# Fused attention and two MLPs on one core: other token chunks, weight decoding on another engine, a new written order

## The chip, the cores and the metric

The kernel runs on one core of a Trainium2 chip. The core has a matrix engine (PE; its weight loads are told apart as PEld), a vector engine (DVE), an activation engine (ACT), a general engine (POOL) and a queue that issues DMAs (SP). Each takes its instructions strictly in the order in which they stand in its own queue; semaphores join the queues. The metric is the device time of one execution in microseconds (us). Three runs of the kernel before took 647.95, 648.45 and 654.52; the median is 648.45.

## The reference

Three layers follow each other; all is float32, but `moe_w_in` and `moe_w_out` arrive as float64.

```python
# attention: q, k, v of shape (2, 8, 576, 64)
q_d, k_d, v_d = means over groups of 4 positions          # 144 of them
out_d   = softmax(q_d k_d^T / 8) v_d, each row repeated 4 times
out_loc = softmax(q k^T / 8, only where |i - j| < 4) v
x = (out_d + out_loc), as 1152 tokens x 512
# first MLP: w_in 512 x 2048, w_out 2048 x 512
h = x @ w_in;  x = (h * sigmoid(h)) @ w_out
# four experts: w1 512 x 1024, w2 1024 x 512 each, p = normalised domain_probs
out = sum over e of p[:, e] * (relu(x @ w1[e]) @ w2[e])
```

## The kernel before, in words

**Products.** Every float32 operand of the two MLPs is split into a high and a low part (fp32r tiles), and each product is three matmuls: high by high, high by low, low by high (`mm3`, L601). A weight tile is 128x128; the moving operand is a chunk of tokens.

**Attention** is 16 jobs of 256 or 320 tokens (two batches, two token halves, four pairs of heads), each a chain over several engines. The program has a name for every step: S (local scores, PE), x (row maximum and subtraction, DVE), e (exp, ACT), D (scores of the averaged positions, PE), n (their maximum, DVE), d (their exp, ACT), u (row sums, DVE), r and g (normalising, DVE and ACT), T (transposes, PE), a (copies, ACT), V (products with the values, PE), o, f, h, l (the two parts of x). k, v, p, tp are sums over four positions on POOL, q the same on DVE. M are the first matmuls of the first MLP.

**First MLP.** The 2048 hidden columns are done in two halves (hf 0 and 1) of 1024. Each half goes over four chunks of tokens. For a chunk, G (8 column tiles x 4 depth steps x 3 matmuls = 96) makes h; th, gf, gh, gl evacuate it (tanh on ACT, product on DVE, the two parts on ACT and DVE); H (4 x 8 x 3 = 96 matmuls) multiplies with `w_out`; ya adds it to the result. G2_3_1 is chunk 2, column tile 3, depth step 1; chunks 4 to 7 are those of the second half. Chunks 0 and 1 of the first half are worked in `quarter` (L660), so that they can begin while attention still runs; the others in the loop at L1054. Three banks of PSUM (`mm_p`, L68) hold sums.

**Weights of the first MLP** come as float64, in 32 pieces of 128x512 (s0 to s31, 512 KB each) into three staging buffers (`stg_p`, L75; a few in `acc`). `split_raw` (L226) turns a piece into its two float32 parts: A (ACT) rescales the high word into a tile `dec`; B (DVE, a shift) or Z (ACT, from the upper half of the low word) makes the three bits that are missing; C (DVE) joins them; w (ACT) makes the high part, L (POOL) the low part by a difference. B is used for the pieces in `LOW_ON_DVE` (L55), Z for the others. Pieces 0 to 15 serve the first half and 16 to 31 the second.

**The order.** The order on each engine up to the second half is written out by hand: five lists of step names (`WRITTEN`, L931), for SP, PE, ACT, DVE and POOL. Each step of a list is made to follow the one before it on its engine. DMAs have eight completion semaphores in turn, so an issue in SP's queue waits until the DMA eight places earlier or more on the same semaphore has landed.

**Experts** follow (L808 to L928). Nothing of them is changed.

Of the kernel before, what the change touches and what calls it, by code (L numbers as in the profile page):

```python
# [62 lines left out]
def attention_moe_kernel(ctx, tc, kqa, kqb, qtl, va, vb, w64, w1d, w2d, dpr, out):  # L63
# [596 lines left out]
    def quarter(ci, p, o, n):  # L660
        c = slice(o, o + n)
        g = [4 * ci + i for i in range(4)]
        two = n == 256
# [15 lines left out]
        for sums in groups:
            first = {}  # L680
            for i in range(4):
                wh, wl = parts(2 + p, i)
                for d, ps in sums:
                    if not two or len(sums) == 4:
                        next_step(0.125)
                    s = slice(d * 128, d * 128 + 128)
                    h, l = gh[g[i]][:, 0:n], gl[g[i]][:, 0:n]
                    for x, (a, y) in enumerate(((wh, h), (wh, l), (wl, h))):
                        z = two and d % 2
                        m = PE.matmul(out=ps[:, 0:n], lhsT=a[:, s], rhs=y, start=(not z and i == 0 and x == 0),  # L690
                                      stop=(i == 3 and x == 2), skip_group_check=True)
                        if i == 0 and x == 0:
                            first[d] = m
                            if z:
                                after(m, first[d - 1])
                        mark(f"H{ci}_{d}_{4 * p + i}", m)
                if i:
                    attn_tick()
            for d, ps in sums:
                ya = acc[:, d * NT + o:d * NT + o + n]  # L700
                if p == 0:
                    i = ACT.activation(out=ya, in_=ps[:, 0:n], func=ACTF.Copy, scale=0.5)
                else:
                    i = DVE.scalar_tensor_tensor(out=ya, in0=ps[:, 0:n], scalar=0.5, in1=ya, op0=ALU.mult, op1=ALU.add)
                mark(f"ya{ci}_{d}_{p}", i)
# [192 lines left out]
    def outputs(e, ci, ch, p):  # L898
# [33 lines left out]
        """in_kq0 in_kq1 in_s0 in_kq2 in_vg0 in_kq3 in_vg1 in_kq4 in_kq5 in_vw0 in_s1 in_qt in_vg3 in_vw1 in_s3 in_vg2 in_vw2  # L932
        in_s2 in_kq6 in_s8 in_s10 in_vw3 in_kq7 in_s9 in_vg8 in_vw4 in_kq12 in_vw5 in_kq8 in_s11 in_vg9 in_kq9 in_s4
        in_vw6 in_vw7 in_kq10 in_kq11 in_s5 in_vw8 in_s6 in_vw9 in_vg10 in_vg11 in_kq13 in_vw10 in_s7 in_vw11 in_s12
        in_s13 in_qt1 in_kq14 in_s14 in_s15 in_kq15 in_s16 in_s17 in_vw12 in_s18 in_vw13 in_vw14 in_vw15 in_s19 in_s20
        in_s21 in_s22 in_s23 in_pr in_s24 in_s25 in_s26 in_s27 in_s28 in_s29 in_s30 in_s31 in_w8_0 in_w8_1 in_w9_0""",
        """S0 S1 D0 D1 S2 S3 T0 D2 S4 V0 S5 T1 D3 D5 D4 V1 M0 T2 M1 V2 T3 tD S6 T4 V3 D6 S7 M2 tT M3 V4 T5 D7 S8 T6 V5 D8
        H0_0_0 H0_2_0 H0_3_0 S9 H0_1_0 H0_0_1 H0_2_1 V6 T7 G1_0_0 H0_1_1 D9 H0_3_1 G1_0_1 G1_0_2 V7 S10 H0_0_2 H0_2_2 T8
        H0_3_2 G1_0_3 S11 H0_2_3 H0_3_3 H0_1_2 G1_1_0 G1_1_1 D10 G1_1_2 G1_1_3 H0_0_3 V8 T9 D11 G1_2_0 G1_2_1 G1_2_2
        G1_3_0 G1_2_3 H0_1_3 G1_3_1 G1_3_2 G1_3_3 S12 H1_0_0 H1_0_1 H1_1_0 V9 T10 H1_1_1 H1_2_0 H1_2_1 H1_2_2 H1_0_2  # L940
        H1_0_3 H1_2_3 H1_1_2 H1_1_3 H1_3_0 G0_4_0 H1_3_1 G0_4_1 G0_4_2 H1_3_2 D12 G0_4_3 G0_5_0 G0_5_1 G0_5_2 H1_3_3 V10
        S13 G0_5_3 G0_6_0 G0_6_1 G0_7_0 G0_6_2 G0_6_3 G0_7_1 T11 H0_0_4 H0_2_4 G0_7_2 H0_1_4 G0_7_3 V11 T12 utD D13 G1_4_0
        G1_4_1 G1_4_2 G1_4_3 S14 H0_0_5 H0_3_4 G1_5_0 H0_1_5 H0_2_5 H0_0_6 H0_1_6 G1_5_1 G1_5_2 H0_3_5 G1_5_3 H0_2_6 S15
        H0_3_6 H0_0_7 H0_2_7 G1_6_0 H0_3_7 G1_6_1 H0_1_7 utT D15 D14 G1_6_2 G1_6_3 G1_7_0 G1_7_1 G1_7_2 G1_7_3 H1_0_4 V12
        T13 H1_1_4 H1_1_5 H1_0_5 H1_2_4 H1_2_5 H1_1_6 H1_0_6 H1_1_7 H1_2_6 H1_2_7 H1_3_4 H1_0_7 G2_0_0 G2_0_1 G2_0_2
        G2_1_0 G2_0_3 V13 T14 G2_1_1 G2_1_2 G2_1_3 G2_2_0 H1_3_5 G2_2_1 G2_2_2 G2_2_3 H1_3_6 V14 T15 G2_3_0 G2_4_0 G2_3_1
        G2_3_2 G2_4_1 H1_3_7 G2_4_2 G2_3_3 G2_4_3 V15 G2_5_0 G2_5_1 G2_5_2 G2_6_0 G2_7_0 G2_5_3 G2_7_1 G2_7_2 G2_6_1
        G2_6_2 G2_6_3 H2_0_0 H2_0_1 H2_0_2 G2_7_3 H2_1_0 H2_1_1 H2_0_3 H2_1_2 H2_1_3 H2_1_4 H2_0_4 H2_2_0 H2_0_5 H2_2_1
        H2_1_5 H2_0_6 H2_1_6 H2_2_2 H2_2_3 H2_2_4 H2_1_7 H2_0_7 H2_2_5 H2_3_0 H2_3_1 G3_0_0 H2_3_2 H2_2_6 H2_2_7 H2_3_3
        G3_0_1 H2_3_4 G3_0_2 G3_0_3 G3_1_0 H2_3_5 G3_1_1 G3_1_2 G3_1_3 G3_2_0 G3_2_1 G3_2_2 H2_3_6 G3_3_0 G3_2_3 H2_3_7  # L950
        G3_3_1 G3_3_2 G3_3_3 G3_4_0 G3_4_1 G3_4_2 G3_4_3 G3_5_0 G3_5_1 G3_5_2 G3_5_3 G3_6_0 G3_6_1 G3_6_2 G3_7_0 G3_7_1
        G3_6_3 G3_7_2 H3_0_0 G3_7_3 H3_0_1 H3_1_0 H3_0_2 H3_1_1 H3_1_2 H3_0_3 H3_0_4 H3_1_3 H3_2_0 H3_1_4 H3_2_1 H3_2_2
        H3_2_3 H3_1_5 H3_0_5 H3_0_6 H3_1_6 H3_0_7 H3_1_7 H3_2_4 H3_2_5 H3_2_6 H3_3_0 H3_2_7 H3_3_1 G4_0_0 G4_0_1 G4_0_2
        G4_0_3 H3_3_2 G4_1_0 H3_3_3 G4_1_1 G4_1_2 H3_3_4 H3_3_5 H3_3_6 G4_1_3 G4_2_0 H3_3_7 G4_2_1 G4_2_2 G4_2_3 G4_3_0
        G4_4_0 G4_3_1 G4_3_2 G4_3_3 G4_5_0 G4_5_1 G4_4_1 G4_4_2 G4_5_2 G4_5_3 G4_4_3 G4_6_0 G4_6_1 G4_6_2 G4_6_3 G4_7_0
        G4_7_1 H4_0_0 H4_0_1 H4_0_2 G4_7_2 H4_1_0 H4_1_1 G4_7_3 H4_0_3 H4_1_2 H4_0_4 H4_1_3 H4_0_5 H4_2_0 H4_0_6 H4_2_1
        H4_0_7 H4_1_4 H4_2_2 H4_1_5 H4_3_0 H4_3_1 H4_1_6 H4_3_2 H4_2_3 H4_3_3 H4_2_4 H4_1_7 H4_3_4 H4_2_5 H4_3_5 H4_3_6
        H4_2_6 H4_2_7 H4_3_7""",
# [243 lines left out]
```

## Time and profile before

| | |
|---|---|
| median of three runs | 648.45 us |
| the profiled execution | 649.48 us |
| its span (first to last instruction) | 647.7 us |
| PE busy | 629.0 us, 97% of the span |
| DVE, ACT, POOL busy | 64%, 50%, 38% |
| chain that ended last | PE 94%, DVE 3%, ACT 2%, DMA 1% |

The profile's page gives busy times and a chain of work followed back from the last instruction. Matmuls are pipelined: one lasts longer than the distance to the next, so the pace of PE is read from start to start, or from a run of matmuls in the chain divided by their number. A row of a timeline gives the start, the length, the engine, the line, what is written and read, the shape, how many instructions were merged, and in brackets the engine's idle time before it and what ended it.

### The profile page before, as it was taken

To read this page: it belongs to the slowest core of one execution; us is meant where nothing else is said; L and a number is where in the kernel's file an instruction comes from. 1 tells how busy PE (TensorE), PEld (TensorE's weight loads), DVE (VectorE), ACT (ScalarE), POOL (GpSimd) and SP (SyncE) were. 2 spreads that over 40 slices of the span, in tenths; PEclk is the share of its full clock that TensorE was granted. 3 is DMA by queue.
4 is the path that set the end of the run, shared out by engine and by line. 5 is a ranking of instruction groups with operands and counts; after the bars stand their busy time and mean duration, and the time that the engine had idled before them with its cause. 6 is when DMAs were issued, how large, how long until landed. Compare 5 with 4: busy or idle time off the path is not lost.

```text
span 647.7 us, 13723 instructions
## 1 busy us (share of the span) xinstructions
PE 629.0 (97%) x5492; PEld 617.6 (95%) x5492; DVE 415.4 (64%) x859; ACT 325.3 (50%) x746; POOL 249.1 (38%) x353
## 2 busy tenths in 40 slices
...
GB/s 276 285 164 187 175 173 56 78 100 163 194 2 1 132 1 1 162 67 2 1 34 108 113 9 1 1 67 131 66 1 2 1 66 1 1 33 35 2 32 50
DMA packets 16928, 48.17 MB, mean 74 GB/s; under 512 B 2976, under 2 KB 4256, under 8 KB 16864
## 3 DMA queue, kind: packets, MB, share of 16 engines
...
## 4 chain that ended last, share of the span: by engine, by line
PE 94%; DVE 3%; ACT 2%; DMA 1%; issue 0%; POOL 0%; ACTq 0%
PE mm L603 57%; PE p L864 27%; PE mm L690 4%; PE s L403 2%; PE o L522 1%; PE t L490 1%; PE o L518 1%; DVE acc L892 1%; DMA kq<-in_kqa_dram 1%; PE mm L993 1%; PE s L410 1%; PE s L448 0%; PE t L492 0%; ACT dec L236 0%; PE mm L403 0%
## 5 line engine op out<-in xcount | busy, mean ns | idle before, releaser
L603 PE MATMUL mm<-xh,wbuf 128*128 128x256 f32 (+2 forms) x1248 | 259.6, 292 | 0.0
L603 PEld LDWEIGHTS mm<-xh,wbuf 128*128 128x128 f32 x1248 | 203.7, 188 | 0.1
L603 PE MATMUL mm<-xl,wbuf 128*128 128x256 f32 (+2 forms) x624 | 182.0, 292 | 0.0
L849 POOL TENSOR_TENSOR r<-r 128x128 f32<-128x128 f32 x160 | 95.0, 606 | 177.4 <-ACT r L843 133.1
L852 DVE TENSOR_TENSOR h<-r,h 128x384 fp32r<-128x384 f32 (+1 forms) x128 | 91.6, 718 | 65.7 <-ACT h L851 65.4
L851 ACT ACTIVATE h<-r 128x384 fp32r<-128x384 f32 (+1 forms) x128 | 73.3, 578 | 93.5 <-POOL r L849 54.5
L603 PEld LDWEIGHTS mm<-xl,wbuf 128*128 128x128 f32 x624 | 117.1, 188 | 0.0
L864 PE MATMUL p<-wext,h 128*128 128x256 f32 x672 | 89.2, 276 | 0.0
L864 PE MATMUL p<-wbuf,h 128*128 128x256 f32 x672 | 82.7, 276 | 0.0
L864 PEld LDWEIGHTS p<-wext,h 128*128 128x128 f32 x672 | 82.2, 188 | 0.0
L864 PEld LDWEIGHTS p<-wbuf,h 128*128 128x128 f32 x672 | 79.4, 188 | 0.0
L603 PE MATMUL mm<-gh,wbuf 128*128 128x256 f32 (+2 forms) x384 | 77.1, 292 | 0.0
L603 PEld LDWEIGHTS mm<-gh,wbuf 128*128 128x128 f32 x384 | 62.0, 188 | 0.0
L843 ACT ACTIVATE r<-mm 128x512 f32<-128x512 f32 x48 | 28.6, 596 | 65.4 <-PE mm L603 64.7
L849 DVE TENSOR_TENSOR r<-r 128x128 f32<-128x128 f32 x96 | 39.3, 410 | 34.0 <-ACT r L843 29.4
L603 PE MATMUL mm<-gl,wbuf 128*128 128x256 f32 (+2 forms) x192 | 55.8, 291 | 0.0
L631 DVE TENSOR_TENSOR gl<-gf,gh 128x256 fp32r<-128x256 f32 (+2 forms) x64 | 34.2, 540 | 18.1 <-ACT gh L630 17.7
L625 DVE SCALAR_TENSOR_TENSOR gf<-th,mm 128x256 f32<-128x256 f32 (+2 forms) x64 | 28.7, 451 | 23.6 <-ACT th L624 21.6
L251 POOL TENSOR_TENSOR wbuf<-dec,wbuf 128x512 fp32r<-128x512 f32 x24 | 31.0, 1301 | 26.4 <-ACT wbuf L250 20.4
L892 DVE SCALAR_TENSOR_TENSOR acc<-p,pr,acc 128x256 f32<-128x256 f32 (+1 forms) x63 | 36.1, 605 | 3.6 <-PE p L864 3.0
L794 POOL TENSOR_TENSOR wext<-kst,wext 128x512 fp32r<-128x512 f32 x8 | 10.4, 1300 | 69.5 <-ACT wext L792 46.9
L630 ACT ACTIVATE gh<-gf 128x256 fp32r<-128x256 f32 (+2 forms) x64 | 28.0, 442 | 16.5 <-DVE gf L625 15.7
(173 smaller groups left out, 1035.2 us busy)
## 6 DMA issues: line engine op xcount, KB each, us to landing
...
```

The costliest lines, as they stand in the source:

```text
L251: mark(f"L{4 * u + j}", POOL.tensor_tensor(out=l, in0=d, in1=h.bitcast(F32), op=ALU.subtract))
L603: ins = [PE.matmul(out=ps, lhsT=l, rhs=r, start=(first and i == 0), stop=(last and i == n - 1)) for i, (l, r) in enumerate(pairs)]
L625: mark(f"gf{c}_{ft}", DVE.scalar_tensor_tensor(out=gf[:, 0:n], in0=th[:, 0:n], scalar=1.0, in1=ps[:, 0:n], op0=ALU.add, op1=ALU.mult))
L630: latest[ACT] = mark(f"gh{c}_{ft}", ACT.activation(out=gh[g][:, 0:n], in_=gf[:, 0:n], func=ACTF.Copy))
L631: latest[DVE] = mark(f"gl{c}_{ft}", DVE.tensor_tensor(out=gl[g][:, 0:n], in0=gf[:, 0:n], in1=gh[g][:, 0:n].bitcast(F32), op=ALU.subtract))
L690: m = PE.matmul(out=ps[:, 0:n], lhsT=a[:, s], rhs=y, start=(not z and i == 0 and x == 0), stop=(i == 3 and x == 2), skip_group_check=True)
L843: ACT.activation(out=r[:, 0:4].rearrange("p s t -> p (s t)"), in_=ps[:, 0:512], func=ACTF.Relu)
L849: latest[eng] = eng.tensor_tensor(out=r[:, o], in0=r[:, a], in1=r[:, b], op=op)
L851: ACT.activation(out=h, in_=r[:, part], func=ACTF.Copy)
L852: latest[DVE] = DVE.tensor_tensor(out=l, in0=r[:, part], in1=h.bitcast(F32), op=ALU.subtract)
L864: ins = [PE.matmul(out=ps, lhsT=x, rhs=y, start=(opens and k == 0 and i == 0), stop=(k == 3 and i == n - 1), skip_group_check=True) for i, ...
L892: DVE.scalar_tensor_tensor(out=o, in0=ps, scalar=p, in1=o, op0=ALU.mult, op1=ALU.add)
```

## The change

1. `CHUNKS`: both halves now use chunks of 256, 256, 256 and 384 tokens; the first half had 256, 320, 256 and 320. `quarter` loses its code for 320 tokens: both its chunks sum two column blocks in one PSUM bank. The pools of gh, gl, th and gf are 256 wide until the last chunk of the first half, and 384 wide from there (they were 320 wide until the second half).
2. `LOW_ON_DVE` has pieces 16 to 31 too: their missing bits are made by the shift B on DVE, and Z leaves ACT. For these pieces `dec` is no tile of its own any more: A writes over the high word in the staging buffer, and C, w and L work there.
3. The five lists of `WRITTEN` are new.

```diff
-XN = (256, 320, 256, 320)
-CHUNKS = (tuple(zip(XOFF, XN)), ((0, 256), (256, 256), (512, 256), (768, 384)))
+CHUNKS = ((0, 256), (256, 256), (512, 256), (768, 384))
...
-LOW_ON_DVE = (0, 1, 2, 3)
+LOW_ON_DVE = (0, 1, 2, 3) + tuple(range(16, 32))
...
-            d = d_p.tile([128, 512], F32, tag="dec", name="dec")
+            d = d_p.tile([128, 512], F32, tag="dec", name="dec") if u < 4 else v[:, :, 1].bitcast(F32)
...
-        if two:
-            b = [mm_tile() for _ in range(2)]
-            groups = [[(d, half(b[d // 2], d % 2)) for d in range(4)]]
-        else:
-            groups = [[(d, mm_tile()) for d in ds] for ds in ((0, 1, 2), (3,))]
+        b = [mm_tile() for _ in range(2)]
+        sums = [half(b[d // 2], d % 2) for d in range(4)]
...
-        """in_kq0 in_kq1 in_s0 in_kq2 in_vg0 in_kq3 in_vg1 in_kq4 in_kq5 in_vw0 in_s1 in_qt in_vg3 in_vw1 in_s3 in_vg2 in_vw2
+        """in_kq0 in_kq1 in_s0 in_kq2 in_kq3 in_vg0 in_s1 in_kq4 in_s2 in_vg1 in_vw0 in_vw1 in_qt in_kq5 in_vw2 in_vw3 in_vg2
...
-        """e0 A0 e1 d0 d1 e2 g0 a0 tab w0 o0 d2 g1 e3 A1 h0 e4 e5 a1 w1 d3 o1 d4 g2 h1 a2 d5 g3 A2 g4 A3 o2 a3 Z8 w3 h2 g5
+        """tab e0 A0 d0 g0 e1 w0 e2 A1 a0 e3 d1 g1 d2 o0 e4 w1 h0 a1 d3 d4 g2 e5 o1 a2 h1 Z10 A2 d5 g4 g3 o2 a3 A3 g5 w2 h2
...
+            if hf == 0 and lastc:
+                m1ctx.close()
+                open_g(384)
```

The built programs show what the new lists do. ACT at the start of the program, before:

```order
L424 ACT_TABLE_LOAD
L424 ACTIVATE s<-s 128x280
L236 ACTIVATE dec<-stg_136 128x512
L424 ACTIVATE s<-s 128x280
L465 ACTIVATE ed,s<-s,stf 128x144 x2
L424 ACTIVATE mm<-mm 128x280
L480 ACTIVATE ed<-ed,stf 128x144
```

and after:

```order
L294 ACT_TABLE_LOAD
L294 ACTIVATE qdl<-zero 128x128
L422 ACTIVATE s<-s 128x280
L234 ACTIVATE dec<-stg_136 128x512
L463 ACTIVATE ed,s<-s,stf 128x144
L478 ACTIVATE ed<-ed,stf 128x144
L422 ACTIVATE s<-s 128x280
```

A small fill of `qdl`, which needs only a zeroed column, now stands first; the load of the table goes with it, ahead of the first exp (e0) and no longer behind job 0's maximum. Job 0's d and g stand ahead of job 1's exp.

SP at the start (kq: keys and queries of a job, stg: a weight piece, vg and vw: values, qt: queries of the tail), before:

```order
L128 DMA kq<-in_kqa_dram 128x838 x2
L128 DMA stg_136<-in_w_dram 128x512
L128 DMA kq_f<-in_kqa_dram 128x838
L128 DMA vg_f_147<-in_va_dram 72x1024
L128 DMA acc<-in_kqa_dram 128x838
L128 DMA vg_f_153<-in_va_dram 72x1024
L128 DMA kq<-in_kqb_dram 128x646 x2
L128 DMA vw<-in_va_dram 72x512
L128 DMA stg_138<-in_w_dram 128x512
```

and after:

```order
L126 DMA kq<-in_kqa_dram 128x838 x2
L126 DMA stg_136<-in_w_dram 128x512
L126 DMA kq_f<-in_kqa_dram 128x838
L126 DMA acc<-in_kqa_dram 128x838
L126 DMA vg_f_147<-in_va_dram 72x1024
L126 DMA stg_138<-in_w_dram 128x512
L126 DMA kq<-in_kqb_dram 128x646
L126 DMA stg_140<-in_w_dram 128x512
L126 DMA vg_f_153<-in_va_dram 72x1024
L126 DMA vw<-in_va_dram 72x512 x2
```

Pieces s1 and s2 moved ahead of the values vw0 of job 0; kq5 moved behind them.

DVE up to f0 (the L527 or L525 instruction, which makes job 0's part of x), before:

```order
L478 TENSOR_TENSOR sm<-s,stf 128x280
L418 TENSOR_REDUCE stf<-mm 128x4
L419 TENSOR_TENSOR mm<-mm,stf 128x280
L463 TENSOR_REDUCE stf<-mm 128x1
L464 TENSOR_SCALAR stf<-stf 128x1
L418 TENSOR_REDUCE st<-s 128x5
L419 TENSOR_TENSOR s<-s,st 128x350
L527 TENSOR_TENSOR o<-o,od 128x256
L427 TENSOR_REDUCE mm<-mm 128x4
L239 TENSOR_SCALAR stg_138<-stg_138 128x512
```

and after:

```order
L242 SCALAR_TENSOR_TENSOR dec<-dec,stg_138 128x512
L237 TENSOR_SCALAR stg_140<-stg_140 128x512
L425 TENSOR_REDUCE s<-s 128x4
L461 TENSOR_REDUCE stf<-mm 128x1
L462 TENSOR_SCALAR stf<-stf 128x1
L469 TENSOR_SCALAR s<-s 128x5
L470 RECIPROCAL stf<-s 128x5
L476 TENSOR_TENSOR sm<-s,stf 128x280
L416 TENSOR_REDUCE st<-s 128x5
L417 TENSOR_TENSOR s<-s,st 128x350
L425 TENSOR_REDUCE mm<-mm 128x4
L525 TENSOR_TENSOR o<-o,od 128x256
```

The decoding of pieces 1 and 2 (B and C at L237 and L242, here of stg_138 and stg_140) stood behind f0 and now stands ahead of it; B2 is the L237 row of stg_140.

## Rows read from the trace of the kernel before

**Rows 1.** Stages: window, length, busy (count) by engine, PE clock, DMA share, GB/s.

```profile
4.00:24.00 20.00, 15.21 (x162) 11.31 (x162) 14.19 (x37) 8.05 (x22) 12.04 (x23) 0.83 0.99 296
24.00:42.00 18.00, 15.65 (x197) 13.96 (x195) 15.35 (x48) 15.13 (x44) 13.72 (x18) 0.91 0.68 226
42.00:130.00 88.00, 87.35 (x1001) 82.03 (x1000) 61.68 (x160) 65.18 (x182) 34.85 (x53) 1.00 0.44 136
130.00:175.00 45.00, 45.00 (x339) 44.96 (x339) 23.16 (x40) 35.76 (x74) 20.63 (x16) 1.00 0.51 156
```

**Rows 2.** Timeline of PE: S0, D0, T0, V0's value products, M0, M3's last.

```profile
4.37 1.20 PE L403 MATMUL s<-kq 64*64 64x70 f32 x16 [4.37 <-DMA kq<-in_kqa_dram]
...
8.76 0.74 PE L444 MATMUL s<-kd,qp 64*64 64x144 f32 x4 [1.37 <-ACT s L424]
...
15.02 0.63 PE L490 MATMUL t<-ident,sm 128*70 128x128 f32 x4 [1.88 <-DVE sm L478]
...
19.97 1.07 PE L522 MATMUL o<-at,vw 70*64 70x64 f32 x16
...
26.15 0.39 PE L993 MATMUL mm<-xh,wbuf 128*128 128x256 f32 x1
...
42.26 0.28 PE L993 MATMUL mm<-xh,wbuf 128*128 128x256 f32 x1
```

**Rows 3.** The chain: start, length, work; matmuls of 320, 256 and 384 columns.

```profile
108.57 5.29 PE mm L690 x36
...
302.90 2.72 PE mm L603 x24
...
328.40 4.16 PE mm L603 x24
```

**Rows 4.** Groups by form: the first and last of six with 320-column matmuls.

```profile
L603 PE MATMUL mm<-xh,wbuf 128*128 128x320 f32 x128 | 32.0, 312 | 0.0
...
L690 PE MATMUL mm<-gl,wbuf 128*128 128x320 f32 x32 | 10.0, 312 | 0.0
```

**Rows 5.** Lines L239 (B) and L244 (C): count, least, median and greatest ns.

```profile
L239 DVE TENSOR_SCALAR stg<-stg x3: 421/426/1241, 10.0 to 32.1; 128x512 int32<-128x512 int32 x3
...
L244 DVE SCALAR_TENSOR_TENSOR dec<-dec,stg x29: 679/691/1565, 11.4 to 171.6; 128x512 int32<-128x512 int32 x29
```

**Rows 6.** Groups by form: Z, A and L.

```profile
L251 POOL TENSOR_TENSOR wbuf<-dec,wbuf 128x512 fp32r<-128x512 f32 x24 | 31.0, 1301 | 26.4 <-ACT wbuf L250 20.4 <-DVE st L463 5.5
...
L236 ACT ACTIVATE dec<-stg 128x512 f32<-128x512 f32 x29 | 19.4, 669 | 1.8 <-POOL wext L251 0.8 <-DMA stg<-in_w_dram 0.3 <-POOL wbuf L251 0.3
...
L242 ACT ACTIVATE stg<-stg 128x512 int32<-128x512 uint16 x26 | 17.4, 674 | 2.2 <-DMA stg<-in_w_dram 2.2
```

**Rows 7.** Timeline of ACT: the table load.

```profile
6.97 1.28 ACT L424 ACT_TABLE_LOAD   x1 [6.97 <-DVE s L419]
```

**Rows 8.** Timeline of SP: the issues of s1 and of s2.

```profile
7.30 0.33 SPq L128 DMA_DIRECT2D stg<-in_w_dram  x1
...
15.49 0.35 SPq L128 DMA_DIRECT2D stg<-in_w_dram  x1
```

**Rows 9.** Timeline of DVE: f0, x6's second instruction, l3.

```profile
21.34 0.43 DVE L527 TENSOR_TENSOR o<-o,od 128x256 f32<-128x256 f32 x1 [0.66 <-ACT od L525]
...
34.64 0.53 DVE L419 TENSOR_TENSOR s<-s,st 128x350 f32<-128x350 f32 x1
...
38.13 0.41 DVE L535 TENSOR_TENSOR xl<-o,xh 128x256 fp32r<-128x256 f32 x1
```

**Rows 10.** Timelines of PE, from a matmul of H to one of V.

```profile
51.19 0.28 PE L690 MATMUL mm<-gh,wbuf 128*128 128x256 f32 x1
51.40 0.50 PE L518 MATMUL o<-atd,vd 72*64 72x80 f32 x8
```

**Rows 11.** Timelines of POOL and DVE at 10 us: a value sum beside B0.

```profile
9.96 1.04 POOL L342 TENSOR_TENSOR vg_f<-vg_f 72x512 f32<-72x512 f32 x1 [1.52 <-DMA vg_f<-in_va_dram]
...
10.04 1.24 DVE L239 TENSOR_SCALAR stg<-stg 128x512 int32<-128x512 int32 x1
```

More of the change, by code (lines that the diff above doesn't have):

```diff
@@ L672, in quarter @@
         flush()
-        if two:
-            b = [mm_tile() for _ in range(2)]
-            groups = [[(d, half(b[d // 2], d % 2)) for d in range(4)]]
-        else:
-            groups = [[(d, mm_tile()) for d in ds] for ds in ((0, 1, 2), (3,))]
-        step[0] -= 0.5
[L679 to L705, printed above, removed]
@@ new lines, in quarter @@
+        b = [mm_tile() for _ in range(2)]
+        sums = [half(b[d // 2], d % 2) for d in range(4)]
+        step[0] -= 0.5
+        first = {}
+        for i in range(4):
+            wh, wl = parts(2 + p, i)
+            for d, ps in enumerate(sums):
+                next_step(0.125)
+                s = slice(d * 128, d * 128 + 128)
+                h, l = gh[g[i]], gl[g[i]]
+                for x, (a, y) in enumerate(((wh, h), (wh, l), (wl, h))):
+                    m = PE.matmul(out=ps, lhsT=a[:, s], rhs=y, start=(d % 2 == 0 and i == 0 and x == 0),
+                                  stop=(i == 3 and x == 2), skip_group_check=True)
+                    if i == 0 and x == 0:
+                        first[d] = m
+                        if d % 2:
+                            after(m, first[d - 1])
+                    mark(f"H{ci}_{d}_{4 * p + i}", m)
+            if i:
+                attn_tick()
@@ L707, in g2_evac @@
+        for d, ps in enumerate(sums):
+            ya = acc[:, d * NT + o:d * NT + o + n]
+            if p == 0:
+                i = ACT.activation(out=ya, in_=ps, func=ACTF.Copy, scale=0.5)
+            else:
+                i = DVE.scalar_tensor_tensor(out=ya, in0=ps, scalar=0.5, in1=ya, op0=ALU.mult, op1=ALU.add)
+            mark(f"ya{ci}_{d}_{p}", i)
     def g2_evac(hf, db, c, ps, n):
@@ L936, in attention_moe_kernel @@
[L936 to L940, printed above, removed]
@@ new lines, in attention_moe_kernel @@
+        G4_4_0 G4_4_1 G4_4_2 H3_3_4 G4_5_0 G4_5_1 G4_5_2 G4_5_3 G4_4_3 H3_3_5 H3_3_6 H3_3_7 G4_6_0 G4_6_1 G4_6_2 G4_6_3
+        G4_7_0 G4_7_1 G4_7_2 G4_7_3 H4_0_0 H4_0_1 H4_0_2 H4_1_0 H4_1_1 H4_1_2 H4_0_3 H4_2_0 H4_1_3 H4_2_1 H4_0_4 H4_1_4
+        H4_2_2 H4_1_5 H4_0_5 H4_0_6 H4_1_6 H4_0_7 H4_1_7 H4_2_3 H4_2_4 H4_3_0 H4_3_1 G5_0_0 G5_0_1 H4_2_5 H4_3_2 H4_2_6
+        H4_2_7 H4_3_3 H4_3_4 H4_3_5 H4_3_6 H4_3_7 G5_1_0 G5_0_2 G5_1_1 G5_0_3 G5_2_0 G5_2_1 G5_1_2 G5_2_2 G5_3_0 G5_3_1
+        G5_3_2 G5_3_3 G5_1_3 G5_2_3""",
@@ new lines, in attention_moe_kernel @@
+        th4_3 w28 gh4_3 A30 th4_4 th4_5 A29 gh4_5 ya3_3 w29 th4_6 gh4_4 A31 gh4_6 w30 th4_7 w31 gh4_7 yh4_1 yh4_2 yh4_0
+        th5_0 th5_1 yh4_3 gh5_0 th5_2 gh5_1 th5_3 gh5_2""",
+        """cz q0 q1 x0 B0 x1 n0 C0 u0 r0 q2 x2 B1 x3 n1 C1 B2 u1 n2 r1 x4 u2 q3 f0 r2 n3 n4 l0 x5 u3 u4 f1 r4 n5 l1 r3 u5 r5
+        f2 C2 x6 nt0 l2 B3 C3 rt0 C8 n6 f3 x7 l3 u6 r6 gf0_0 C9 C10 f4 x8 gl0_0 l4 n7 gf0_1 u7 gf0_2 r7 f5 gl0_1 gf0_3 l5
+        n8 x9 C11 f6 l6 u8 r8 n9 gl0_3 gl0_2 f7 x10 l7 gf1_0 u9 r9 C5 C4 n10 f8 gf1_1 x11 gl1_1 gl1_0 u10 l8 r10 n11 gf1_2
@@ new lines, in attention_moe_kernel @@
+        C22 C23 gf3_6 gl3_5 gf3_7 C24 gl3_6 B26 B25 gl3_7 C25 C26 B27 C27 gf4_0 gf4_1 gl4_1 gf4_2 B28 C28 gl4_0 gf4_3 B30
+        gl4_2 B29 gl4_3 gf4_4 gf4_5 C29 gl4_5 C30 gf4_6 B31 gl4_4 C31 gf4_7 gl4_6 gl4_7 yf4_0 yf4_1 yl4_1 yf4_2 yl4_0
+        yf4_3 yl4_2 gf5_0 yl4_3 gf5_1 gl5_1 gf5_2 gl5_2 gf5_3 gl5_0""",
+        """cb cm ci k0 k1 cq k2 v0 k3 p4 v1 tp L0 p5 v2 L1 v3 p6 L2 L3 p7 L8 v8 p8 L9 v9 p9 L10 L11 p10 v10 p11 L5 L4 L6 L7
+        p13 p12 v11 utp L12 L13 p14 L14 L15 p15 L16 L18 L17 L21 L20 L19 L22 L23 L24 L25 L26 L27 L28 L29 L30 L31""",
@@ L1015, in attention_moe_kernel @@
     first_ctx.close()
-    open_g(320)
+    open_g(256)
     def split_ok(limit):
```

92 lines of the change are left out of this document (40 added, 52 removed).

## The prediction, made before the changed kernel was run

> **What bounds the kernel now.** I read the stages first, since a mean over the span hides them [rows 1]. From 130 to 175 us PE is busy for all of 45.00 us; from 42 to 130 it lacks 0.65 of 88. Only before 42 us does it stand still: it is busy for 15.21 of the 20 us from 4 to 24 and for 15.65 of the 18 that follow, so 4.79 + 2.35 = 7.14 us are idle there, of which 0.37 belong to the wait for the first load, which ends at 4.37 [rows 2]. So the kernel has two regimes. After 42 us, PE's own pace sets the end, and what another engine saves is worth nothing until PE waits for it. Before 42 us, chains over all engines set it, and at most some 6.8 us of idle time lie there, beside the 4.4 us of the first load that no order removes. The timeline of PE names the stops: D0 waited for an exp (1.37 us), T0 for the normalising on DVE (1.88) [rows 2]. The stage column also shows a granted clock of 0.83 and 0.91 there, against 1.00 later: part of the time at the lower of its two levels.
>
> **Part 1, the chunks.** The matmuls stay the same in number and in columns: a weight tile meets 1152 tokens in four chunks either way. What counts is the pace by width, which the chain shows where matmuls run unbroken [rows 3]: 5.29/36 = 146.9 ns at 320 columns, 2.72/24 = 113.3 at 256, 4.16/24 = 173.3 at 384. The two 320-column chunks hold 2 x (96 + 96) = 384 matmuls, which is what the six groups of that width add up to (the first has 128, the last 32) [rows 4]. They become 192 of 256 and 192 of 384: 384 x 146.9 = 56.42 us before, 192 x (113.3 + 173.3) = 55.03 after. That is **-1.39 us**, on the path, since PE has no idle time to lose it in. The Trainium skill (TensorE: Matmul & The Clock Gate, Back-to-back issue gap) gives a warm matmul a gap of its columns at 2.4 GHz plus a fixed 2.5 ns; by that, equal columns and an equal count cost the same, this term is 0 and the result 1.4 us later. The rows above disagree: the excess over the columns' own time (106.7, 133.3 and 160.0 ns at that rate) is 6.6, 13.6 and 13.3 ns, not fixed. I take the rows.
>
> **Part 2, the decoding of pieces 16 to 31.** ACT loses 16 Z of 674 ns, 10.8 us; DVE gains 16 B, 0.43 us each when nothing disturbs them, 6.8 us [rows 5, 6]. Both happen mostly between 130 and 175 us, where ACT is busy for 35.76 of 45 us and DVE for 23.16, and PE is full all the same [rows 1]. So neither the relief nor the load is on the path: **0**. The cover is the 21.8 us that DVE has idle there; when it is gone, gf comes late and PE runs out of PSUM banks (the first rival). Writing `dec` in place makes every second word the operand. I price that at 0: Z reads and writes with that stride already and costs 674 ns, against 669 for A, which writes without [rows 6]; below 0 it cannot be. The staging buffer is now held until L is done, 1.3 us behind w [rows 6], where it was free after C. Pieces are loaded ahead of use, and POOL, where L runs, is busy for 20.63 of 45 us [rows 1], so this is 0 too.
>
> **Part 3, the new order at the start.** Three edits matter.
> - The table load of 1.28 us stood between x0 and e0, waiting for DVE [rows 7]. It now waits for nothing, so e0, D0 and T0 can come 1.3 us earlier. On DVE, q0 and q1 run while PE still works on S0, and d0, g0 go ahead of e1. T0 may gain some 3 us.
> - Against that stands the load order. The issue of s1 at 7.30 us waited for s0, that of s2 at 15.49 for vw0: eight semaphores in turn [rows 8]. By the shapes, 1350 KB had landed at the first and 3554 at the second: 2204 KB in 8.19 us, 269 KB/us, and the DMA engines are 0.99 busy from 4 to 24 us [rows 1]. Now s1 and s2 stand ahead of vw0, and 4255 KB come in up to it: 7.30 + (4255 - 1350)/269 = 18.1 us. V0 cannot multiply with the values before that; before it did so at 19.97 [rows 2]. Everything on PE behind V0 (T1, D3, D4, S5) waits with it. So 1.9 us of the gain at T0 get through, not 3.
> - From f0 to l3 DVE is nearly full: 16.8 us from 21.34 to 38.13 [rows 9]. B1, C1 and B2 (0.43 + 0.69 + 0.43 = 1.55 us [rows 5]) leave this stretch for the time in which DVE waits for V0; the maximum of job 7, two instructions of about 0.53 [rows 9], enters it. That is 0.5 us more, so l3, on which M3 hangs, comes 2.4 us earlier.
>
> M0 (26.15 us) and M3's end (42.26) [rows 2] should move by about that. I take **-2.5 us**. The bounds are +1 (the later values, with nothing won elsewhere) and -6.8 (all idle time that an order can remove); the value lies nearer to the row of V0, since PE must pass that step in order.
>
> The new list for PE has 53 changes between matmuls of the MLP and those of attention, against 51. Such a change costs 51.40 - 51.19 = 0.21 us instead of the 0.113 of the pace, some 0.1 us [rows 3, 10]: **+0.2 us**.
>
> **Sum**, against the profiled execution of 649.48 us: 649.48 - 1.39 - 2.5 + 0.2 = 645.8. That execution was 1.03 above the median of 648.45, so the forecast in the terms of the median is **644.7 us**, 0.6% less. I call 1% (6.5 us) what a measurement of this kernel can tell from no change; the forecast is within it.
>
> **Rivals.**
> 1. *DVE becomes the bound between 130 and 175 us* (slower). B0 took 1.24 us beside a value sum on POOL that ran from 9.96 to 11.00, against 0.43 alone, and the longest C 1.57 against 0.69 [rows 5, 11]. L on POOL runs in the same stretch as the new B. If each B and each C meets an L, DVE gets 16 x (1.24 + 1.57 - 0.69) = 33.9 us more, 57.0 in a stretch that holds 45 us of PE's work plus 192 x (173.3 - 146.9) ns = 5.1 for the wider last chunk: 7 us over. The time would be 644.7 + 7 = 652. It decides from 27 us of extra DVE time, when four in five pieces meet an L. Against it: all but a few of the 29 C took 0.69, with 16 L in the same stretch. Chance 0.07. The Trainium skill (SBUF — State Buffer, Who interferes with whom) says that DVE and GpSimd share a pair of ports under an exclusive lock, that tensor_scalar and two-input operations can need it, and that the second to come is blocked until the first ends. B0's row agrees with it; by that rule alone a new B would be held up whenever an L is running, which is this rival.
> 2. *The start gives nothing*: the later values and a full DVE leave M3 where it was. Only the chunks remain: 648.45 - 1.39 + 0.2 = 647.3 us. For it: M3 hangs on l3, and DVE was 15.35 of 18 us busy [rows 1]. Chance 0.20.
> 3. *The start gives nearly all its idle time*: V0's wait is shorter than by my estimate of the load rate, and the earlier T0 pulls all the rest. 648.45 - 1.39 - 6.8 + 0.2 = 640.5 us at the end of this case, 642 at its beginning. For it: ACT is busy for only 8.05 of the 20 us from 4 to 24 [rows 1], so there is room. Chance 0.18.
> 4. The forecast, 642 to 646.5: 0.55.
>
> **From these to the numbers.** Under 642.0 lie rival 3 and a little of the forecast's edge: faster by over 1%, 0.20. Over 654.9 only rival 1 with the start lost as well: 0.03. The rest, 0.77, is within 1%. For 8 in 10 I cut the far end of rival 3 and all of rival 1 but its mildest form: 640.8 to 648.6.
>
> **What would show it.** Right: matmuls of 113 and 173 ns only and none of 147; the table load before 5 us; T0 before 13 us; V0's second part at about 18 us, ended by a DMA of vw; M0 at 23 to 24.5 and M3's end at 39 to 40.5 us; PE full from there to the experts, with ACT some 11 us less busy and DVE some 7 more. Wrong: PE idle between 130 and 200 us with gf as what ended it (rival 1); M3's end at 42 (rival 2) or before 37 us (rival 3); a stop of PE later than 42 us that is not in the trace of before.

## The result: 0.6% slower, where 0.6% faster was forecast

The changed kernel takes 652.45 us (median of 22 runs, 647.84 to 658.49), the kernel before beside it 648.15 us (22 runs). The ratio is **1.0057, 95% interval 1.0032 to 1.0082**: 3.7 us slower. The forecast was 644.7 us with a range of 640.8 to 648.6; time and sign are both wrong, though the difference stays within the 1% that I called no change. The profiled execution took 649.11 us (span 647.3), which is near the low end of its runs: its trace need not show all that the median holds. Here and below a median is over all executions, while a ratio leaves out those more than 1.5% above the fastest of the same kernel.

### The profile page after: what moved, and what is told of

It reads as the page before. It is cut to its first block, busy times and chain, and to the rows that moved or that the text cites. A ratio compares the mean times of both kernels' runs of the same rounds, so it can differ in the third digit from the quotient of the medians.

```text
span 647.3 us, 13746 instructions
## 1 busy us (share of the span) xinstructions
PE 627.0 (97%) x5492; PEld 615.9 (95%) x5492; DVE 421.8 (65%) x875; ACT 316.2 (49%) x730; POOL 251.0 (39%) x353
## 4 chain that ended last, share of the span: by engine, by line
PE 88%; DVE 4%; DMA 3%; ACT 2%; issue 1%; POOL 1%; POOLq 0%; ACTq 0%; DVEq 0%
PE mm L601 52%; PE p L855 27%; PE mm L681 3%; DMA stg<-in_w_dram 2%; PE s L401 1%; PE t L488 1%; PE o L520 1%; PE o L516 1%; POOL u L249 1%; DMA kq<-in_kqa_dram 1%; DVE acc L883 1%; DVE gl L629 1%; DVE dec L242 0%; PE s L408 0%; PE s L446 0%
## 5 line engine op out<-in xcount | busy, mean ns | idle before, releaser
L601 PE MATMUL mm<-xh,wbuf 128*128 128x256 f32 (+1 forms) x1248 | 258.6, 292 | 0.0
L601 PE MATMUL mm<-xl,wbuf 128*128 128x256 f32 (+1 forms) x624 | 181.8, 291 | 0.0
L601 PE MATMUL mm<-gh,wbuf 128*128 128x256 f32 (+1 forms) x384 | 79.3, 297 | 0.0
L601 PE MATMUL mm<-gl,wbuf 128*128 128x256 f32 (+1 forms) x192 | 56.7, 296 | 1.3 <-DVE gl L629 1.3
L629 DVE TENSOR_TENSOR gl<-gf,gh 128x256 fp32r<-128x256 f32 (+1 forms) x64 | 36.0, 572 | 13.3 <-ACT gh L628 12.6
L623 DVE SCALAR_TENSOR_TENSOR gf<-th,mm 128x256 f32<-128x256 f32 (+1 forms) x64 | 28.5, 451 | 20.8 <-ACT th L622 19.5
L601 PEld LDWEIGHTS mm<-gl,wbuf 128*128 128x128 f32 x192 | 36.0, 188 | 1.6 <-DVE gl L629 1.6
L622 ACT ACTIVATE th<-mm 128x256 f32<-128x256 f32 (+1 forms) x64 | 25.9, 410 | 19.9 <-PE mm L601 19.4
L628 ACT ACTIVATE gh<-gf 128x256 fp32r<-128x256 f32 (+1 forms) x64 | 27.5, 442 | 12.9 <-DVE gf L623 12.8
```

The costliest lines, as they stand in the source:

```text
L601: ins = [PE.matmul(out=ps, lhsT=l, rhs=r, start=(first and i == 0), stop=(last and i == n - 1)) for i, (l, r) in enumerate(pairs)]
L622: mark(f"th{c}_{ft}", ACT.activation(out=th[:, 0:n], in_=ps[:, 0:n], func=ACTF.Tanh, scale=0.5))
L623: mark(f"gf{c}_{ft}", DVE.scalar_tensor_tensor(out=gf[:, 0:n], in0=th[:, 0:n], scalar=1.0, in1=ps[:, 0:n], op0=ALU.add, op1=ALU.mult))
L628: latest[ACT] = mark(f"gh{c}_{ft}", ACT.activation(out=gh[g][:, 0:n], in_=gf[:, 0:n], func=ACTF.Copy))
L629: latest[DVE] = mark(f"gl{c}_{ft}", DVE.tensor_tensor(out=gl[g][:, 0:n], in0=gf[:, 0:n], in1=gh[g][:, 0:n].bitcast(F32), op=ALU.subtract))
```

## The profile after

The stages again, for the changed kernel, with one more at the end (columns as in [rows 1]):

```profile
4.00:24.00 20.00, 15.98 (x189) 11.80 (x190) 16.72 (x47) 9.73 (x29) 15.01 (x30) 0.82 1.00 335
24.00:42.00 18.00, 17.43 (x226) 15.53 (x225) 16.00 (x42) 15.54 (x44) 12.44 (x17) 0.92 0.80 260
42.00:130.00 88.00, 85.79 (x1017) 81.82 (x1017) 62.04 (x167) 62.69 (x179) 36.48 (x55) 1.00 0.36 112
130.00:175.00 45.00, 43.69 (x285) 43.02 (x285) 23.27 (x43) 24.18 (x52) 14.74 (x11) 1.00 0.45 137
...
175.00:215.00 40.00, 38.59 (x335) 38.39 (x335) 23.58 (x50) 18.28 (x42) 4.22 (x3) 1.00 0.24 73
```

The last stage in before:

```profile
175.00:215.00 40.00, 39.96 (x353) 39.77 (x352) 20.54 (x48) 16.98 (x40) 0.00 (x0) 1.00 0.09 27
```

Before 42 us PE is busy for 2.55 us more than in [rows 1]. From 42 to 215 us it stood still for 0.69 us in all (0.65 of them before 130 us); in the three stages it now lacks 2.21, 1.31 and 1.41 us. The timeline of PE in the changed kernel names the places: first T0, V0's product with vw, T1, M0 and M3's last, which answer to [rows 2], then four stops that the trace of before does not have:

```profile
11.14 0.63 PE L488 MATMUL t<-ident,sm 128*70 128x128 f32 x4 [0.45 <-DVE sm L476]
...
16.09 0.69 PE L520 MATMUL o<-at,vw 70*64 70x64 f32 x16 [1.41 <-DMA vw<-in_va_dram]
17.48 1.04 PE L488 MATMUL t<-ident,sm 128*70 128x128 f32 x4 [0.70 <-DVE sm L476]
...
25.46 0.59 PE L986 MATMUL mm<-xh,wbuf 128*128 128x256 f32 x1
...
39.06 0.28 PE L986 MATMUL mm<-xh,wbuf 128*128 128x256 f32 x1
...
43.49 0.39 PE L681 MATMUL mm<-gl,wbuf 128*128 128x256 f32 x1 [1.14 <-DVE gl L629]
...
55.81 0.39 PE L681 MATMUL mm<-gl,wbuf 128*128 128x256 f32 x1 [1.07 <-DVE gl L629]
...
161.18 0.44 PE L601 MATMUL mm<-gl,wbuf 128*128 128x384 f32 x1 [1.31 <-DVE gl L629]
...
197.69 0.39 PE L601 MATMUL mm<-xh,u 128*128 128x256 f32 x1 [1.41 <-DVE gf L623]
```

The four stops add up to 4.93 us. M3 ends 3.20 us earlier than in [rows 2], and the stop of 0.65 us that before had is gone. With the 1.39 us forecast for the chunks these sum to -0.31 us, and the traced executions differ by -0.37 (649.11 and 649.48). So the two traces fit four stops that ate the gain; they do not show why the median is 4.3 us higher. The chain of waits of the changed kernel shows how the stop at 161 us comes about; its first row is a run of H at 256 columns:

```profile
104.96 2.72 PE mm L681 x24
...
142.80 1.28 POOL wext L249
...
144.10 4.71 DMA stg<-in_w_dram
...
152.93 1.64 POOL u L249
154.59 5.21 DMA stg<-in_w_dram
...
159.89 0.10 DVE stg L237
...
160.66 0.48 DVE gl L629
161.13 0.04 issue
161.18 8.86 PE mm L601 x62
```

L on POOL ends (the L249 rows), and only then can the next piece be loaded into that staging buffer (4.71 and 5.21 us from issue to landing). The load lands at 159.8, and two B stand ahead of gl in DVE's queue. The timelines of ACT and DVE there, and DVE's waits from 120 to 200 us (total, times, longest):

```profile
155.71 0.93 ACT L628 ACTIVATE gh<-gf 128x384 fp32r<-128x384 f32 x2
```

```profile
156.26 1.37 DVE L629 TENSOR_TENSOR gl<-gf,gh 128x384 fp32r<-128x384 f32 x1 [1.15 <-ACT gh L628]
159.89 0.76 DVE L237 TENSOR_SCALAR stg<-stg 128x512 int32<-128x512 int32 x2 [2.27 <-DMA stg<-in_w_dram]
160.57 0.55 DVE L629 TENSOR_TENSOR gl<-gf,gh 128x384 fp32r<-128x384 f32 x1
```

```profile
DVE stg L237 <- DMA stg<-in_w_dram: 9.7, 5, 3.8
```

In the trace of before, DVE waits for no DMA in that stretch. DVE had time for the new B (busy for 23.27 of the 45 us from 130 on), but its queue is served in order: the gh that gl reads was made by 156.64 us, and gl ran at 160.57, behind two B whose data had not come.

## The experiments

Each was timed against the kernel before on the same chip; "ratio" is to that, with its 95% interval.

**The same kernel again.** Median 650.57 us, ratio 1.0049 [1.0018, 1.0080]; its trace (649.41 us) has the same four stops (1.17, 1.07, 1.64 and 1.41 us).

> The changed kernel once more, for its spread and a second trace. Theory 1 (staging): pieces 16 to 31 now hold their staging buffer until the low part is made, the next load starts late, B on DVE waits for it, and gf and gl queue behind B; so a trace slower than the first one (649.1 us) shows the extra time as stops of PE between 125 and 200 us, ended by DVE, 4 to 8 us in all; median 651 to 654. Rival (start): the extra time lies before 60 us, where values and keys land late; stops after 125 us stay at 3 us.

**B as late as possible**, directly ahead of its C:

```diff
-B20 B21 C21 C20 B19 C19 ... gl3_6 B26 B25 gl3_7 C25 C26
+B21 C21 B20 C20 B19 C19 ... gl3_6 gl3_7 B25 C25 B26 C26
```

> Only the written list of DVE differs from the changed kernel: each B of pieces 16 to 31 stands directly ahead of its C, no longer several steps earlier. Theory 1: DVE waits less for landings in front of gf and gl, 1 to 3 us off the copy beside it, and the stops of PE after 125 us shrink. Rival (start): no difference, within 1 us of the copy.

656.85 us, 1.0103 [1.0064, 1.0142]: not faster than the copy, rather slower. In its trace the stop at 161 us went, others came (0.46 at 140.96 us behind ACT's ya, 0.65 at 143.96 behind gf, 1.05 at 185.76 and 1.41 at 201.38). From 130 to 215 us PE lacks 3.58 us there, where after lacks 2.72: moving the waits chose other victims. Some 4 us more of this trace are a slower pace of PE behind 200 us (last section).

**A fourth staging buffer, with its control.** It fits only if th and gf share tiles and two spacer tiles go, so the control has these alone.

```diff
-gf = tmp_p[0].tile([128, tmp_p[1]], F32, tag="gf", name="gf")
+gf = th
...
-stg_p = ctx.enter_context(tc.tile_pool(name="stg", bufs=3, side="right"))
+stg_p = ctx.enter_context(tc.tile_pool(name="stg", bufs=4, side="right"))
```

> A control for the next one: th and gf share one tile (three of them, where there were two of each) and two filler tiles are left out; staging as in the changed kernel. Both theories: within 1 us of the copy.

> As the control, with four staging buffers for three. Theory 1: the loads of pieces 16 to 31 start one piece earlier, B no longer waits, PE has no stop over 0.5 us between 125 and 200 us: 4 to 7 us off the control, 645 to 648. Rival (start): what is lost before 60 us stays, at most 1.5 us off the control.

Control 662.99 us (4 runs), 1.0225 [1.0186, 1.0264]; with the fourth buffer 660.38 (5 runs), 1.0183 [1.0148, 1.0219]: 2.6 us less, where 4 to 7 were expected. The stop at 161 us (1.85 us in the control) is gone, and DVE's waits for loads from 120 to 200 us fall from 10.7 to 2.8 us. The holding of buffers is part of that stop. That the control itself is 2% slower, against its expectation, lies mostly in a slower pace of PE behind 180 us (last section).

**Part 2 alone, in the order of before.** Three kernels were meant to have the hold, B, and both:

```diff
-d = d_p.tile([128, 512], F32, tag="dec", name="dec")
+d = d_p.tile([128, 512], F32, tag="dec", name="dec") if u < 16 else v[:, :, 1].bitcast(F32)
...
-LOW_ON_DVE = (0, 1, 2, 3)
+LOW_ON_DVE = (0, 1, 2, 3) + tuple(range(16, 32))
-C16 ... C31
+B16 C16 ... B31 C31
```

> The kernel before, with one line changed: pieces 16 to 31 are decoded in their staging buffer, which is so held until L is done; Z stays on ACT, the chunks and all five lists are those of before. Theory 1 (the hold costs): the loads of pieces 19 to 31 are issued later than the 147 to 167 us of before, A on ACT then waits for a DMA, th and gh queue behind it, and PE gets stops between 130 and 200 us that before did not have; time 1 to 5 us above before. Theory 2 (B on DVE costs, not the hold): as before within 0.5 us, no new stop of PE. Theory 3 (only the start costs): as before within 0.5 us.

> The kernel before, with B of pieces 16 to 31 on DVE, each directly ahead of its C, and no Z for them on ACT; the tile dec stays, so the staging buffer is free after C as before. 16 x 0.43 = 6.9 us more on DVE, 16 x 0.67 = 10.8 us less on ACT. Theory 1 (the hold costs): as before within 0.7 us, no new stop of PE. Theory 2 (B on DVE delays gf and gl): stops of PE between 130 and 200 us with gf or gl as what ended them, time 2 to 6 us above before. Theory 3 (only the start costs): as before within 0.5 us.

> The kernel before with both: pieces 16 to 31 decoded in their staging buffer, and B on DVE directly ahead of C. Theory 1 (the hold costs): late loads as with the hold alone, but now DVE waits for them too, gf and gl queue behind; 2 to 6 us above before, stops of PE between 130 and 200 us. Theory 2: as with B alone. Theory 3 (only the start costs): as before within 0.5 us.

The first edit changes nothing. In it `u` counts units of four pieces and runs from 0 to 7 for these weights, so `u < 16` always holds (after has `u < 4`). The trace agrees: with that edit all 29 A of staged pieces still write into `dec`, as in before, where in after 16 of them write into the staging buffer. Groups by form, the kernel meant as the hold alone and after:

```profile
L236 ACT ACTIVATE dec<-stg 128x512 f32<-128x512 f32 x29 | 19.4, 669 | 1.7 <-POOL wext L251 0.8 <-POOL wbuf L251 0.3 <-POOL u L251 0.3
```

```profile
L234 ACT ACTIVATE stg<-stg 128x512 f32<-128x512 f32 x16 | 10.6, 677 | 6.7 <-DMA stg<-in_w_dram 6.7
```

So these were before once more, B alone, and B alone once more:

| | median us | ratio |
|---|---|---|
| before once more | 648.37 | 1.0010 [0.9978, 1.0042] |
| B alone | 650.09 | 1.0033 [1.0005, 1.0062] |
| B alone once more | 651.39 | 1.0050 [1.0017, 1.0084] |

The hold alone was not measured in this order, and my first theory (the hold costs) is tested only in the order of after. B alone costs 0.3 and 0.5%. From 130 to 200 us before once more has no new stop; B alone makes two, 0.95 and 0.46 us in the one trace and 0.94 and 1.32 in the other. Timelines of POOL, DVE and PE in the first trace of B alone:

```profile
147.21 1.30 POOL L251 TENSOR_TENSOR u<-dec,u 128x512 fp32r<-128x512 f32 x1 [4.69 <-ACT u L250]
```

```profile
147.31 1.75 DVE L244 SCALAR_TENSOR_TENSOR dec<-dec,stg 128x512 int32<-128x512 int32 x1
148.98 0.47 DVE L625 SCALAR_TENSOR_TENSOR gf<-th,mm 128x320 f32<-128x320 f32 x1
```

```profile
149.51 0.41 PE L603 MATMUL mm<-xh,wbuf 128*128 128x320 f32 x1 [0.95 <-DVE gf L625]
...
173.74 0.38 PE L603 MATMUL mm<-xh,wext 128*128 128x256 f32 x1 [0.46 <-DVE gf L625]
```

The two B ahead of it moved this C onto an L of POOL; it took 1.75 us instead of 0.69, gf came late behind it, and PE stood. The Trainium skill (SBUF — State Buffer, Who interferes with whom) describes such a mutual exclusion of DVE and GpSimd, for a DVE instruction with two SBUF inputs beside a GpSimd one that reads SBUF. The row agrees: C ends at 149.06 us, 0.55 behind the end of L.

**Z on ACT again, in the order of after** (the hold stays):

```diff
-LOW_ON_DVE = (0, 1, 2, 3) + tuple(range(16, 32))
+LOW_ON_DVE = (0, 1, 2, 3)
-A18 ... A17 ... A16
+A18 Z18 ... A17 Z17 ... A16 Z16
```

> The kernel after, with the missing bits of pieces 16 to 31 made by Z on ACT again, Z directly behind A, and no B for them on DVE; decoding in the staging buffer, chunks and the rest of the order as in after. Theory 1 (B on DVE puts the wait for a late load, and B's own time, ahead of gf and gl in DVE's queue; the hold alone is harmless): the stop of PE at 161 us is gone or under 0.3 us, DVE waits for no DMA of stg; 1 to 2.5 us below after. Theory 2 (the hold alone makes the loads late, whoever decodes): the stop at 161 stays above 0.8 us, since A and Z on ACT then hold up gh and th; no gain, or a loss up to 2 us. The stops at 43, 56 and 198 us stay under both.

654.30 us, 1.0090 [1.0051, 1.0128]. In its trace (665.80 us, with the slower pace of the last section from 184 us on) the stop at 161 us is gone and DVE waits for no load, as theory 1 had it; the gain did not come. Timelines of ACT and PE:

```profile
135.22 0.68 ACT L234 ACTIVATE stg<-stg 128x512 f32<-128x512 f32 x1 [2.91 <-DMA stg<-in_w_dram]
...
138.59 0.36 ACT L702 ACTIVATE acc<-mm 128x256 f32<-128x256 f32 x1
```

```profile
139.00 0.44 PE L601 MATMUL mm<-xh,wbuf 128*128 128x384 f32 x1 [0.91 <-ACT acc L702]
```

Now ACT waits 2.91 us for the load and works off three pieces, and ya, which frees a bank of PSUM, stands behind. So B is not the cause by itself: with the hold a load comes late here too, and it harms whichever queue waits for it, if something that PE needs stands behind.

**The stops removed by moves in the lists alone** (chunks, hold and B as in after):

```diff
-H0_0_0 V5 T6          (PE)
+V5 T6 H0_0_0
-H0_2_2 T8             (PE)
+T8 H0_2_2
-gl0_3 gl0_2           (DVE)
+gl0_2 gl0_3
-B26 B25 gl3_7         (DVE)
+gl3_7 B26 B25
-th5_1 yh4_3           (ACT)
+yh4_3 th5_1
```

> The kernel after, with five moves in its lists at its four new stops of PE: H0_0_0 behind V5 and T6, T8 ahead of H0_2_2, gl0_2 ahead of gl0_3, gl3_7 ahead of B26 and B25, and yh4_3 ahead of th5_1 on ACT. Chunks, decoding and all else as in after. If these stops are what the change lost, PE's stops at 43, 56, 161 and 198 us (1.14, 1.07, 1.31 and 1.41 in after) shrink to under 1.5 us together and the time is 3 to 4 us below after. If the loss is elsewhere (start, or a slower pace of PE over long stretches), the stops go and the time stays within 1 us of after.

651.95 us, 1.0020 [0.9992, 1.0049]: some 2.4 us less than after by the ratios, whose intervals overlap. In its trace (663.35 us, with the slower pace from 198 us on) the stop at 43 us is replaced by two, at 40.33 (1.03, a load of vw) and 44.00 (0.99, behind DVE's xl), that at 56 shrank to 0.37, that at 161 became one of 0.79 at 163.23 (ya on ACT behind a w that waits for the same load), that at 198 one of 0.65. With Z on ACT and the first three moves and the last it was 654.35, 1.0067 [1.0041, 1.0094], against its expectation: the stop of PE behind ya, now at 139.85 us, is 1.40 there.

> The kernel after with Z on ACT again for pieces 16 to 31 and the moves at 43, 56 and 198 us: what is left of the change are the chunks, the hold and the new start. If the chunks bring the 1.39 us of the prediction and the start some 1 us, and nothing else costs, it is 1.5 to 3 us below before, and the fastest of all; if B and the four stops were not the loss, it is at or above before.

With three further moves (ya3_0 and ya3_2 ahead of w25; the last G5 steps one column tile at a time; vw0 loaded ahead of s1):

> The kernel after with the five moves of the earlier experiment, vw0 loaded ahead of s1, ya3_0 and ya3_2 ahead of w25 on ACT, and the last G5 steps on PE one column tile at a time. If the stops of PE are what the change lost: no stop over 0.5 us between 130 and 210 us, 1.5 to 3 us below before. If something else costs (the slower pace of PE over long stretches): no stops, yet at before or above.

648.97 us, 0.9993 [0.9958, 1.0028]. Its stages, and DVE's waits for the loads from 120 to 200 us:

```profile
130.00:175.00 45.00, 45.00 (x298) 45.00 (x297) 25.78 (x49) 26.25 (x55) 14.73 (x11) 1.00 0.46 140
175.00:215.00 40.00, 40.00 (x354) 40.00 (x353) 25.28 (x54) 18.73 (x44) 4.26 (x3) 1.00 0.28 86
```

```profile
DVE stg L237 <- DMA stg<-in_w_dram: 8.9, 6, 3.3
```

This settles the two later stops: DVE still waits 8.9 us for late loads, and PE has no idle time at all from 130 to 215 us. (The same lists with added matmuls, below, were traced too, and have no stop above 0.16 us there.) The waits cost nothing once gl, gf and ya stand ahead of them. The profiled execution took 645.60 us, 3.5 less than that of after; 2.72 of these are the two stops. By the ratios the moves are worth 0.64%, some 4.1 us, and the intervals of the two kernels do not overlap. Those at 43 and 56 us were not cured: between 42 and 130 us PE lacks 2.16 us here too (1.77 at 43.99, now for an exp on ACT).

**The start alone**: before, with the lists of after up to M3.

> The kernel before with the lists of after up to and including in_kq7 (SP), M3 (PE), h3 (ACT), l3 (DVE) and L3 (POOL), and the rest of its own lists behind them; chunks and decoding as before. It is the third part of the change alone. By the prediction and theory 1 (the start gains, the hold eats it): M3 ends before 40.5 us, time 2 to 3.5 us below before, as steady as before. Theory 3 (the start of after costs: its values and keys land late in many executions): M3 not earlier, or a time at or above before, with runs spread up to 657 us as those of after.

648.47 us, 0.9999 [0.9966, 1.0032]: nothing that can be measured, although M3 ends at 39.06 us in its trace and at 42.26 in [rows 2]. The reverse, after with the start of before (651.06 us, 1.0032 [0.9993, 1.0070]), says the same:

> The kernel after with the lists of before up to in_kq7 (SP), M3 (PE), h3 (ACT), l3 (DVE) and L3 (POOL): chunks, decoding and the later order of after, start of before. If the new start gives nothing in the median (as alone): as after, 2.5 to 5 us above before, with the stops at 161 and 198 us. If the new start gives its 2.5 us inside after, 5 to 7 us above before. If the new start is what makes after slow, at or below before.

What is wrong is the yardstick. In the second trace of before's own program M3 ends at 39.92 us, in the two of B alone, which have the same start, at 41.17 and 38.83, and in after with the start of before at 39.90. The execution on which I worked was the latest of five. The mean of the five is 40.42; eleven traces with the new start and no added matmuls have 38.50 to 40.97, mean 39.21. So the new start brings some 1.2 us by the traces, half of what I forecast, and an interval of 0.3% (2.1 us) to either side cannot tell that from nothing. V0's wait for vw (2.22 us in the kernel with the start alone) is not the limit either:

```diff
-in_vg0 in_s1 in_kq4 in_s2 in_vg1 in_vw0
+in_vg0 in_vw0 in_s1 in_kq4 in_s2 in_vg1
```

> The kernel before with the lists of after up to M3 as in the experiment on the start, and the load of job 0's values (vw0) moved from behind s2 and kq4 to ahead of s1. If V0's wait for its values (2.22 us in that experiment) is what eats the earlier T0, V0 comes below 15 us, M3 ends before 38.3 us, and the time is 1 to 2 us below before. If the chain behind V0 is set by DVE, M3 ends at 38.5 to 39.5 all the same and the time is as before within 0.7 us.

648.25 us, 0.9995 [0.9969, 1.0022]. V0 ran at 14.42 us, but PE then stood 2.16 us for T1's normalising on DVE, and M3 ended at 38.98: the second case of the expectation.

**PE kept busy through V0's wait**, by 40 more matmuls (80 as the trace counts them), in the kernel with the start alone and in the one with all moves, there with vw0 loaded where after loads it:

```diff
+for _ in range(10 if j.i == 0 else 0):
+    for h in range(2):
+        p = slice(64 * h, 64 * h + 64)
+        for kh in range(2):
+            mark("V0", PE.matmul(out=o[p, 320:320 + nd], lhsT=v[:, kh, p], rhs=j.atd[:, kh, h, :], start=(kh == 0), stop=(kh == 1)))
```

> The kernel of the experiment on the start alone (before with the lists of after up to M3), with 40 matmuls of 64 columns added in front of V0's product with vw, where PE stood still for 2.22 us: they repeat V0's product with vd and write the same numbers again. If the lower clock behind that stop is what eats the start's gain, the granted clock stays above 0.9 from 18 to 26 us, M0 comes below 23.5 us (24.62 before), and the time is 1 to 2.5 us below that experiment's 648.5. If the clock falls all the same, or M3 hangs on DVE anyway, M3 ends at 38.5 to 39.5 us and the time is as there within 0.7 us.

> As the kernel with all moves, but with vw0 where after has it and the 40 added matmuls in front of V0's product with vw. If the stops and the clock are what the change lost, it is 2 to 4 us below before and the fastest of all; if only the stops are, as the kernel with all moves within 1 us.

On the start alone 649.36 us, 1.0012 [0.9978, 1.0045]; on the kernel with all moves 647.96, 0.9971 [0.9932, 1.0010], the lowest of all. It is below after, but not measurably below before, nor below the same kernel without the added matmuls. Busy time and granted clock of PE from 14 to 26 us, in before, in after, in before once more (with the row from 34 us on for both traces of before) and in the last one (its trace: 661.57 us):

```profile
14.00:18.00 4.00, 1.97 (x14) 0.80 0.97 273
18.00:22.00 4.00, 4.00 (x63) 0.50 0.91 248
22.00:26.00 4.00, 3.51 (x47) 0.85 1.03 357
...
34.00:38.00 4.00, 2.39 (x44) 0.86 0.26 62
```

```profile
14.00:18.00 4.00, 1.88 (x28) 0.83 0.90 258
18.00:22.00 4.00, 3.80 (x32) 0.50 1.04 338
22.00:26.00 4.00, 4.00 (x37) 0.50 1.04 349
```

```profile
14.00:18.00 4.00, 4.00 (x37) 1.00 1.01 281
18.00:22.00 4.00, 2.89 (x56) 1.00 1.00 247
22.00:26.00 4.00, 4.00 (x49) 1.00 1.01 248
...
34.00:38.00 4.00, 3.84 (x33) 0.62 0.90 231
```

```profile
14.00:18.00 4.00, 4.00 (x110) 1.00 0.86 231
18.00:22.00 4.00, 2.41 (x29) 1.00 1.02 272
22.00:26.00 4.00, 4.00 (x38) 0.57 1.05 291
```

After stands for more than 2 of the 4 us from 14 on, and then works at 0.50, the lower level (1.2 GHz), for some 8 us: its T1 takes 1.04 us instead of 0.63. "Busy for 4.00 of 4" hides that. Every trace with the new start and no added matmuls has such a stretch (0.50 or 0.63 at its lowest); of the five with the old start before has it, one of B alone has 0.70 for 4 us, and three have 1.00 from 14 to 30 us. The old start meets the lower level later: from 34 to 38 us four of its five traces have 0.57 to 0.86, where all with the new start and no added matmuls have 1.00. The added matmuls kept the full level through 22 us, but PE then stood another 1.12 us and the clock fell behind that; M3 ended at 38.20 us instead of 39.06 in after. On the start alone they did not help: a load of keys came late there (PE stood 2.41 us for it), PE stood again for 1.96 us before 23.00, the clock was 0.50 from 26 to 30 us, and M0 came at 28.25 us, not below 23.5 as expected, and M3's end at 42.44. So one trace puts the lower clock's part at under 1 us, and the times show no gain; how much it costs the new start stays open.

## Why the prediction was wrong, point by point

- **"After 42 us, PE's own pace sets the end"** was true of before, and I carried it over to an order that had been written anew. This step failed: the new order has four stops, 4.93 us, where the sum has nothing but 0.2 us for changes between matmuls. I named the sign ("a stop of PE later than 42 us that is not in the trace of before") and gave it no price. Removing the stops at 161 and 198 us by moves in the lists, with hold and B as they are, brings the time back to that of before (0.9993, though not below it).
- **Part 1** (-1.39): the pace of [rows 3] came at 256 columns, 2.72/24 = 113.3 ns in the chain of after, and no matmul of 320 is left. The sum of the two traces above fits the term; no run shows the chunks alone.
- **Part 2** (0): the work moved as forecast (ACT 9.1 us less busy in the trace, DVE 6.4 more, for about 11 and 7), but the price failed too: "Pieces are loaded ahead of use [...], so this is 0 too". The three staging buffers were no reserve. Held until L, they bring loads 4.7 and 5.2 us long onto the chain, and B carries that wait into the queue in which gf and gl stand: 1.31 us at 161 us. In the order of before, B alone cost 0.3 and 0.5%; what the hold alone costs there, no run shows. "The cover is the 21.8 us that DVE has idle there" was the wrong kind of cover: idle time of a queue in order covers only what nobody behind has to wait for.
- **Part 3** (-2.5): T0 came at 11.14 us (below 13, as said), V0 waited for vw as forecast, but only until 16.09 instead of 18.1. The loads moved at 335 GB/s (4 to 24 us); the 269 KB/us of the estimate, in units of 1024 bytes, are 276. M0 came at 25.46, not at 23 to 24.5, and M3's end at 39.06, within the forecast 39 to 40.5. Yet the start alone measures 0.0% (-0.3 to +0.3). The failed step is the end from which I subtracted: 42.26 us is one execution, and four others with the same start have 38.8 to 41.2.
- **The size of the miss** is 1.15% between the forecast (0.9942 of before; the sum as written gives 644.8 us, not 644.7) and the result, some 7.4 us. The moves that removed stops are worth 4.1 us and the start fell short by up to 2.5; each of these is known to some 2 or 3 us.
- **The rivals.** Rival 2 (the start gives nothing, 0.20) is what the time of the start alone shows, though not by its condition: M3's end moved. Rival 1 had the right place and mechanism in a mild form: one C beside one L (1.75 us) makes a stop of 0.95, long before DVE is the bound. I asked when DVE would be full, and not what a single late gf does.
- **What stays open**: the trace of after accounts for 649.1 us, the median is 652.45. Both traces of after lack the slower pace described at the end, which six other traces with the new lists have; whether its other executions had it, no run shows.
